# Copies, splits and weight conversions around the first two experts of an attention, MoE and FFN kernel in another order

## The chip, the cores and the metric

The kernel runs on one core of one Trainium2 chip. The metric is the device time of one execution in microseconds (us); three runs of a kernel are shown by their median. The engines are named as in the profile: PE is TensorE, PEld its weight loads, DVE VectorE, ACT ScalarE, POOL GpSimd, SP SyncE, which here issues DMAs.

## The reference

Three layers, one after the other, on 2 x 768 tokens of width 384 (8 heads of 48):

```python
for t in range(S):                                     # attention with a decaying state
    state = alpha[:, :, t, :, None] * state + np.einsum('bhd,bhe->bhde', k[:, :, t], v[:, :, t])
    y[:, :, t] = np.einsum('bhd,bhde->bhe', q[:, :, t], state)
...
expert_idx = np.argmax(x @ w_gate, axis=1)             # one of 8 experts per token, 1536 tokens
h = np.maximum(np.einsum('ecd,edf->ecf', disp, w1), 0.0)   # 384 -> 1024
y = np.einsum('ecf,efd->ecd', h, w2)                       # 1024 -> 384
out[i] = gate_w[i] * y[expert_idx[i], pos[i]]
...
h = x @ w_in                                           # second FFN, 384 -> 2048
g = h * np.tanh(np.log1p(np.exp(np.minimum(h, 20.0))))
return g @ w_out                                       # 2048 -> 384
```

All inputs are float32, except that `w_in` and `w_out` of the second FFN come as 64-bit numbers.

## The kernel before, in words

**Stages.** The attention goes over 12 tiles of 128 tokens. Behind each tile its tokens are routed (their expert, their place in it, the gate), scaled by the gate and scattered into a table `tab` in HBM, sorted by expert. Then come the 8 experts, then the second FFN, whose rows are scattered to the output.

**Splits.** Every float32 operand of a product in the experts and in the second FFN is split in two parts: a high part that ACT copies (`whi` of the weights, `xh` of the tokens, `hh` of the middle layer) and a low part that DVE subtracts (`wlo`, `xl`, `hl`). Each product becomes three: high by high, low by high, high by low.

**Weights.** They come in 72 pieces of 128 x 768. SP loads piece i into a staging tile `st` (`load_to`, up to 14 pieces ahead), ACT writes `whi[i]` (`conv_high`, line L343), DVE writes `wlo[i]` (`conv_low`, L349). Pieces 0 to 63 are the experts' (8 each). Pieces 64 to 71 are the first half of the second FFN; these start as 64-bit numbers and are first turned into float32 in 12 jobs. Job n has two halves: `cvt_a(n)` (an ACT copy `wm` at L198, an ACT check at L233, two DVE operations on `wt` at L201 and L204) and `cvt_b(n)` (one DVE operation at L209 that joins the halves of a word, and the DMA that writes the result to `wi_s` or `wo_s` in HBM, L241). Pieces 64 to 71 are then loaded back from there, and a piece's load stands in the program only when the jobs that write it do: pieces 68 to 71 wait for all 12.

**Steps.** An expert e has 8 steps m; step number e*8+m issues `g1(e, m)`, nine products of 240 columns of the first layer (L1100), and `g2` of three steps earlier, nine products of the second layer (L1117). `g1(e, m)` writes a PSUM bank that it shares with `g1(e, m-2)`, so it waits until DVE's `hl(e, m-2)` (L1105) is done. `xpose(e+1)` transposes the next expert's tokens (PE, L1072) and splits them into `xh` and `xl` (L1089, L1090); `gather(e)` fetches them from the table. `place(e)` loads a register with the expert's offset on the engines that address by it.

**Order.** The order in which the program text issues work is the order on each engine: nothing is sorted afterwards. An instruction that waits holds up all that stands behind it on its engine. The conversion halves are put at steps by two lines, in which `CVT_END` is 45 and 24 halves are spread over the list `free`:

```python
free = [s for s in range(3, E * MF) if s % MF != 5 and (s % MF != 2 or s < MF)]
    job_at.setdefault(free[n * CVT_END // (2 * len(cvt_jobs))], []).append(((cvt_a, cvt_b)[n % 2], n // 2))
```

**The check.** Every attention tile leaves in `chk` how far an iteration converged. `check_tiles` (DVE, L784 and L786: `ok`, then `cm`, a minimum over 12 columns) sums it up, `check_all(cm)` at step 7 transposes `cm` on PE (L791) and reduces it on DVE (L793) to a flag, which with the largest expert's count `mxc` decides on a slow path at the end.

**Second FFN.** `f1(n)` is nine products of 512 columns (L1181), from which ACT and DVE make the gated middle layer: a sigmoid, an arctangent and a sine on ACT (`sigma` L1193, then L1197, L1199) and a product and a split on DVE (`gated`: `p` L1209, high part `big` L1210, low part `big` L1211). `f2` is twelve products of 384 columns (L1224) on it. The loop is `f1(n)`, then `f2` of two blocks earlier. Block 4 is the first whose `f1` takes its weights from piece 68.

Of the kernel before, what the change touches and what calls it, by code (L numbers as in the profile page):

```python
# [10 lines left out]
F32 = mybir.dt.float32  # L11
# [12 lines left out]
def kernel(  # L24
# [309 lines left out]

    low = []

    def conv_high(n):
        while conv_n[0] < min(n, len(pieces)):
            i = conv_n[0]
            load_to(i + 1 + ahead[0])  # L340
            w = wst_t.pop(i)
            w_new(i)
            nc.scalar.activation(out=whi[i], in_=w, func=AF.Copy)  # L343
            low.append((i, w))
            conv_n[0] += 1

    def conv_low(only=None):
        for i, w in [x for x in low if only in (None, x[0])]:
# [15 lines left out]

    with ExitStack() as actx:
        ap_ = actx.enter_context(tc.tile_pool(name="att", bufs=1))
        chk = ap_.tile([128, NTILE], F32, name="chk")
        nc.vector.memset(chk, 0.0)
        neg1 = ap_.tile([128, 1], F32, name="neg1")
        nc.vector.memset(neg1, -1.0)  # L370
# [2 lines left out]
        sel = ap_.tile([128, HP, SW], F32, name="sel")  # L373

        tri_f = ap_.tile([128, 128], F32, name="tri_f")
        seen_f = ap_.tile([128, 128], F32, name="seen_f")
        seen = ap_.tile([128, 128], I32, name="seen")
        io_i = ap_.tile([128, E], I32, name="io_i")
        slot_i = ap_.tile([128, WIN], I32, name="slot_i")
# [1 line left out]
        def route_consts():  # L381
            nc.gpsimd.memset(tri_f, 1.0)
            nc.gpsimd.affine_select(
                out=tri_f, in_=tri_f, pattern=[[1, 128]], compare_op=ALU.is_gt,
                fill=0.0, base=0, channel_multiplier=-1,
            )
            nc.gpsimd.memset(ones, 1.0)
            nc.gpsimd.memset(seen_f, -1.0)
            nc.gpsimd.affine_select(
                out=seen_f, in_=seen_f, pattern=[[1, 128]], compare_op=ALU.is_ge,  # L390
                fill=0.0, base=0, channel_multiplier=-1,
            )
            nc.gpsimd.iota(io_i, pattern=[[-1, E]], base=E - 1, channel_multiplier=0)
            nc.gpsimd.iota(slot_i, pattern=[[1, WIN]], base=(E - 1) * NT, channel_multiplier=0)
            nc.gpsimd.iota(tokid, pattern=[[C, NTILE]], base=0, channel_multiplier=1)

        def route_copies():
            nc.scalar.activation(out=tri, in_=tri_f, func=AF.Copy)
            nc.scalar.activation(out=seen, in_=seen_f, func=AF.Copy)
            nc.scalar.activation(out=down, in_=io_i, func=AF.Copy)  # L400
            nc.scalar.activation(out=firsts, in_=io_i[0:1], func=AF.Copy, scale=float(NT))
            nc.scalar.activation(out=slots, in_=slot_i, func=AF.Copy)
# [111 lines left out]

        def k_scale(i):
            kp = sp.tile([128, HP, C], F32, tag="kp", name="kp")
            nc.vector.scalar_tensor_tensor(
                out=kp[0:R2], in0=heads(kn_t.pop(i))[0:R2], scalar=-1.0 if i == NTILE - 1 else 1.0,
                in1=rt_t.pop(i)[0:R2], op0=ALU.mult, op1=ALU.mult,
            )  # L520
            kp_t[i] = kp

        def q_scale(i):
# [410 lines left out]
        for i in range(1, NTILE - 1):  # L934
            far = i + 2 < NTILE
            carry, carried = (t % NC_B != NC_B - 1 for t in (i, i - 1))
            load_step(i + 3)
            zero_tab(i - 1, 4)
            scores(i)
            mask(i, 0)  # L940
            mask(i, 1)
            decay_er(i + 1)
            if i < 7:
                decay_inv(i + 1)
            if carried:
                state_up(i - 1)
            if i >= 7:
                decay_inv(i + 1)
            if carry:
                k_back(i)  # L950
            else:
                idle(i, 1)
            if i in RANK:
                group_rank_mm(RANK[i])
            x_back(i - 1)
            if not far:
                own(RANK[i])
            if carry:
                k_neg(i)
            if i in (7, 8, 9):  # L960
                put(1 + i // 9)
            elif i < 7:
                decay_check(i + 1)
            if far:
                decay_scan(i + 2)
                decay_ln(i + 2)
                group_lg(i - 1)
                decay_exp(i + 2)
                k_scale(i + 1)
                q_scale(i + 1)  # L970
                if i in (7, 8, 9):
                    put(1)
                group_in(i - 1)
                if i in RANK:
                    own(RANK[i])
            else:
                put(2)
                route(i - 1)
                k_scale(i + 1)
                q_scale(i + 1)  # L980
            if i in EXP:
                group_exp(EXP[i])
            if i in HOT:
                group_hot(HOT[i])
            attend_state(i)
            if not carried:
                idle(i, 1)
            attend_tile(i)
            if not far:
                route_rank_mm(i - 1)  # L990
                route_gate(i - 1)
                route_rank(i - 1)
                route_slot(i - 1)
                count(i)
            if carry:
                state_mm(i)
            x_out(i)
            if not far:
                route_x(i - 1)
                route_c(i - 1)  # L1000
            load_to(PRE.get(i, 0))
# [6 lines left out]
        state_up(i - 1)  # L1008
        mask_last(i, 0)
        x_back(i - 1)  # L1010
        idle(i, 2)
        attend_state(i)
        route(i - 1)
        decay_check(i - 1)
# [26 lines left out]
        low_x = split_x(i)  # L1041
        route_rank(i)
        slot_hot(i)
        low_x()
        route_x(i)
        route_slot(i)
        cm = check_tiles()
        count(i + 1)
        route_c(SLOT1)
        conv_high(ATT - 1)  # L1050
        conv_low(0)
        slot_split()
        del xs_t[0]
        tot = rk[:, E:2 * E]
        nc.tensor.matmul(out=tot, lhsT=ones, rhs=pre[pre_n[0] % 2], start=True, stop=True, skip_group_check=True)


    wr_p.append(main.enter_context(tc.tile_pool(name="wr1", bufs=8)))
# [283 lines left out]
    CVT_END = 45  # L1342
    LATE_AHEAD = 3
    xpose(0, False)
    nc.vector.tensor_reduce(out=mxc, in_=tot, axis=AX.X, op=ALU.max)
    conv_low(2)
    conv_high(ATT)
    scatter(tab, si_last, xg_last, E * NT, "tab")
    gather(1)
    pend = []  # L1350
    job_at = {}

    free = [s for s in range(3, E * MF) if s % MF != 5 and (s % MF != 2 or s < MF)]
    for n in range(2 * len(cvt_jobs)):
        job_at.setdefault(free[n * CVT_END // (2 * len(cvt_jobs))], []).append(((cvt_a, cvt_b)[n % 2], n // 2))
    for e in range(E):
        for m in range(MF):
            step = e * MF + m
            if m == 6:
                off_v[e] = place(e)  # L1360
            g1(e, m)
            pend.append((e, m))
            if len(pend) > LAG:
                pe, pm = pend.pop(0)
                g2(pe, pm)
                if pm == MF - 1:
                    y_out(pe)
            if e == E - 1 and m >= MF - EARLY:
                n = m - MF + EARLY
                (f_head if m < MF - 1 else f1_at)(n)  # L1370
# [3 lines left out]
            for f, n in job_at.get(step, ()):  # L1374
                f(n)
                if f is cvt_b:
                    cvt_load(n + 3)
            if step == 4:
                places()
            if step == 5:  # L1380
                sort_places()
            if step == 7:
                check_all(cm)
                slow_at()
            if step % 4 == 3 and 0 < step // 4 <= NTILE:
                tok_scatter(step // 4 - 1)
# [8 lines left out]
            if step == E * MF - 2:  # L1395
                cvt_flag()
            if m == (5 if e else 6) and e + 1 < E:
                xpose(e + 1)
                if e + 2 < E:
                    gather(e + 2)  # L1400
    for pe, pm in pend:
# [242 lines left out]
```

## Time and profile before

| | |
|---|---|
| median of 3 runs | 421.44 us (421.35 to 422.85) |
| the profiled execution | 421.35 us, of which its span, from the first to the last instruction, is 419.6 us |
| mean granted TensorE clock | 0.996 |
| busy: PE, DVE, ACT, POOL | 406.4, 323.9, 324.5, 58.6 us |
| first expert's first product, second expert's first | 75.43 us, 89.94 us |
| first block of the second FFN whose weights are piece 68 | 221.38 us |

The span leaves 1.75 us of the execution outside. The busy times are sums over the whole span, with a matmul's end modelled, so a busy PE says only that something was in it; where it waits is in the timeline, in the idle time before an instruction and what ended it.

### The profile page before, as it was taken

What the parts mean: (1) busy time and instruction counts of PE and PEld (TensorE: products, weight loads), DVE (VectorE), ACT (ScalarE), POOL (GpSimd) and SP (SyncE); (2) the same over time, 40 slices, a digit from 0 to 9 for tenths busy, and PEclk for the clock granted to TensorE, in tenths of its full rate; (3) what the DMA queues carried; (4) which work ended last, traced back from release to release, by engine and by line L of the source; (5) the groups of instructions that cost most, each with busy time, mean ns of one, the idle gap of its engine ahead of it and who ended that gap; (6) DMA issues with size and microseconds to landing.
All of it is one profiled execution on the core that took longest, in us unless ns stands there. A gap on an engine that the chain in (4) does not pass through costs nothing.

```text
span 419.6 us, 8354 instructions
## 1 busy us (share of the span) xinstructions
PE 406.4 (97%) x3111; PEld 374.5 (89%) x3114; DVE 323.9 (77%) x645; ACT 324.5 (77%) x572; POOL 58.6 (14%) x77
## 2 busy tenths in 40 slices
PE   7899999899999999999999999999999999999993
PEld 3798998899999999999999899989898988889893
DVE  7999997899989888988649877867786775565361
ACT  5889997877868677777499987888788869797630
POOL 5222573101101012100000000000000000012043
PEclk9999999999999999999999999999999999999998
DMA  7999996999999999944525000211110000001022
GB/s 236 351 290 334 347 382 224 352 354 235 341 322 285 303 313 283 287 128 125 187 80 174 15 1 0 52 63 39 37 41 1 0 2 0 2 19 57 2 77 80
DMA packets 50541, 67.31 MB, mean 160 GB/s; under 512 B 5372, under 2 KB 41212, under 8 KB 50492
## 3 DMA queue, kind: packets, MB, share of 16 engines
q1 hardware_dynamic: 48572, 61.97, 47.9%
q0 software_dynamic: 1920, 4.73, 3.1%
q8 instruction: 26, 0.43, 0.4%
q14 instruction: 23, 0.19, 0.1%
HBM read 55.86 MB, written 10.83 MB: 159 GB/s over the span
## 4 chain that ended last, share of the span: by engine, by line
PE 89%; DVE 5%; ACT 2%; issue 1%; DMA 1%; POOL 0%; POOLq 0%; DVEq 0%; ACTq 0%
PE bk L1224 24%; PE bk L1181 24%; PE bk L1117 14%; PE bk L1100 14%; PE bk L537 3%; PE bk L589 2%; PE bk L605 2%; PE bk L578 2%; DVE wlo L349 1%; PE bk L557 1%; PE bk L613 1%; PE bk L1072 1%; DMA an<-in_alpha_t_dram 1%; DVE hl L1105 0%; PE bk L868 0%
## 5 line engine op out<-in xcount | busy, mean ns | idle before, releaser
L349 DVE TENSOR_TENSOR wlo<-st,whi 128x768 fp32r<-128x768 f32 x72 | 68.2, 953 | 12.4 <-ACT whi L343 9.9
L1209 DVE TENSOR_TENSOR p<-p,bk 128x512 f32<-128x512 f32 x48 | 32.8, 683 | 43.6 <-ACT p L1199 43.6
L1224 PE MATMUL bk<-whi,big 128*128 128x384 f32 x240 | 66.4, 337 | 0.0
L343 ACT ACTIVATE whi<-st 128x768 fp32r<-128x768 f32 x72 | 60.1, 841 | 0.0
L1193 ACT ACTIVATE p<-bk 128x512 f32<-128x512 f32 x48 | 28.8, 599 | 32.0 <-PE bk L1181 28.6
L1117 PE MATMUL bk<-hl,whi 128*128 128x240 f32 x192 | 52.9, 276 | 0.0
L1117 PE MATMUL bk<-hh,wlo 128*128 128x240 f32 x192 | 52.7, 275 | 0.0
L1117 PE MATMUL bk<-hh,whi 128*128 128x240 f32 x192 | 52.7, 274 | 0.0
L1224 PEld LDWEIGHTS bk<-whi,big 128*128 128x128 f32 x240 | 44.1, 188 | 1.5
L1104 ACT ACTIVATE hh<-bk 128x240 fp32r<-128x240 f32 x64 | 23.5, 367 | 28.2 <-PE bk L1100 25.3
L108 POOL DMA_INDIRECT out_dram<-acc,srt x12 | 12.2, 1018 | 225.5 <-DVE acc L1248 221.1
L1181 PE MATMUL bk<-x2l,whi 128*128 128x512 f32 x144 | 41.6, 397 | 0.0
L1181 PE MATMUL bk<-x2h,wlo 128*128 128x512 f32 x144 | 41.2, 394 | 0.0
L1181 PE MATMUL bk<-x2h,whi 128*128 128x512 f32 x144 | 41.1, 394 | 0.0
L1224 PE MATMUL bk<-wlo,big 128*128 128x384 f32 x120 | 40.6, 338 | 0.0
L1117 PEld LDWEIGHTS bk<-hl,whi 128*128 128x128 f32 x192 | 36.4, 189 | 0.2 <-DVE hl L1105 0.2
L1117 PEld LDWEIGHTS bk<-hh,whi 128*128 128x128 f32 x192 | 36.3, 189 | 0.0
L1117 PEld LDWEIGHTS bk<-hh,wlo 128*128 128x128 f32 x192 | 36.3, 189 | 0.0
L1100 PE MATMUL bk<-xh,whi 128*128 128x240 f32 x192 | 33.0, 280 | 1.7 <-ACT xh L1089 1.6
L1181 PEld LDWEIGHTS bk<-x2h,wlo 128*128 128x128 f32 x144 | 27.0, 188 | 6.7
L1181 PEld LDWEIGHTS bk<-x2l,whi 128*128 128x128 f32 x144 | 27.0, 188 | 6.4
L1100 PE MATMUL bk<-xl,whi 128*128 128x240 f32 x192 | 32.1, 276 | 0.4 <-DVE xl L1090 0.4
(238 smaller groups left out, 955.4 us busy)
## 6 DMA issues: line engine op xcount, KB each, us to landing
st<-in_w_dram SPq DMA_DIRECT2D x64, 384.0 KB, 7.9
qn<-in_q_t_dram SPq DMA_DIRECT2D x12, 256.0 KB, 5.4
kn<-in_k_t_dram SPq DMA_DIRECT2D x12, 256.0 KB, 7.1
w<-in_w_in_dram SPq DMA_DIRECT2D x6, 512.0 KB, 7.4
w<-in_w_out_dram SPq DMA_DIRECT2D x6, 512.0 KB, 6.4
sd<-in_w_in_dram SPq DMA_DIRECT2D x8, 384.0 KB, 4.1
sd<-in_w_out_dram SPq DMA_DIRECT2D x8, 384.0 KB, 4.7
tab<-zero SPq DMA_DIRECT2D x4, 720.0 KB, 6.5
```

What stands on the lines that cost most here:

```text
L108: r = nc.gpsimd.indirect_dma_start(out=dst[:, :], out_offset=bass.IndirectOffsetOnAxis(ap=idx, axis=0), in_=src, in_offset=None, bounds_ch ...
L343: nc.scalar.activation(out=whi[i], in_=w, func=AF.Copy)
L349: nc.vector.tensor_tensor(out=wlo[i], in0=w, in1=whi[i].bitcast(F32), op=ALU.subtract)
L537: nc.tensor.matmul(out=sc_t[i][r][:, j], lhsT=kp[p, j, :], rhs=qq[p, j, :], start=True, stop=True)
L578: nc.tensor.matmul(out=ot_at(j, r), lhsT=s2f[half(r), j * D:j * D + w], rhs=q2[i % 2][half(r), j, :], start=(j % 2 == 0), stop=False, skip ...
L1100: nc.tensor.matmul(out=hps, lhsT=a[:, kk], rhs=b_[:, kk, :], start=(n == 0), stop=(n == 3 * KD - 1))
L1104: nc.scalar.activation(out=hh, in_=hps, func=AF.Relu)
L1117: nc.tensor.matmul(out=y[n], lhsT=a[:, ns], rhs=b_, start=(m == 0 and t == 0 and n % 2 == 0), stop=(m == MF - 1 and t == 2), skip_group_ch ...
L1181: r = nc.tensor.matmul(out=hps, lhsT=a[:, kk], rhs=b_[:, kk, w0:w0 + wd], start=(n == 0), stop=(n == 3 * KD - 1))
L1193: nc.scalar.activation(out=p, in_=h2_t[b], func=AF.Sigmoid, scale=-1.0)
L1209: nc.vector.tensor_tensor(out=g, in0=g, in1=h2_t.pop(b), op=ALU.mult)
L1224: nc.tensor.matmul(out=o_t[c], lhsT=a[:, ts], rhs=b_, start=(m in (0, MA) and n == 0), stop=(m in (MA - 1, MF2 - 1) and n == 2),)
```

## The change

It changes the order of ACT's copies and of DVE's small operations between the attention and the second expert, shifts all conversion halves by two entries of `free`, and has four small edits in the attention. Part by part:

- ACT copies `whi[2]` between the two gate-scaled copies `xg_lh` and `xg_l` of the last tile, `whi[1]` behind `xh` of the first expert, and `whi[3]` behind step 0. Before, `whi[1]` and `whi[2]` stood together in front of `xh`.
- `check_tiles` moves from in front of the first expert to step 7, right ahead of the transposes of its result; `mxc` moves to step 4; the product for `tot` moves behind `g1(0, 0)`.
- `xpose(1)` stands ahead of step 6's weight copies, and `place(0)` a step later.
- The conversion halves start at step 5's place in `free` instead of step 3's: the first, `cvt_a(0)`, goes from step 3 to 6, the last, `cvt_b(11)`, from step 60 to 63 (the last step).
- GpSimd builds the mask `seen` as int32 at once, and ACT's copy to int32 is gone; `k_scale` is a plain product for tiles 1 to 10; tile 9's gate stands ahead of tile 11's `q_scale`; one of the last tile's two keep-busy products, which nothing reads, is gone.

```diff
@@ -334,15 +334,17 @@
+    def high(i):
+        load_to(i + 1 + ahead[0])
+        w = wst_t.pop(i)
+        w_new(i)
+        nc.scalar.activation(out=whi[i], in_=w, func=AF.Copy)
+        low.append((i, w))
+        conv_n[0] += 1
+
     def conv_high(n):
         while conv_n[0] < min(n, len(pieces)):
-            i = conv_n[0]
-            load_to(i + 1 + ahead[0])
-            w = wst_t.pop(i)
-            w_new(i)
-            nc.scalar.activation(out=whi[i], in_=w, func=AF.Copy)
-            low.append((i, w))
-            conv_n[0] += 1
+            high(conv_n[0])
...
-            nc.gpsimd.memset(seen_f, -1.0)
+            nc.gpsimd.memset(seen, -1)
             nc.gpsimd.affine_select(
-                out=seen_f, in_=seen_f, pattern=[[1, 128]], compare_op=ALU.is_ge,
-                fill=0.0, base=0, channel_multiplier=-1,
+                out=seen, in_=seen, pattern=[[1, 128]], compare_op=ALU.is_ge,
+                fill=0, base=0, channel_multiplier=-1,
             )
...
-            nc.scalar.activation(out=seen, in_=seen_f, func=AF.Copy)
...
-            nc.vector.scalar_tensor_tensor(
-                out=kp[0:R2], in0=heads(kn_t.pop(i))[0:R2], scalar=-1.0 if i == NTILE - 1 else 1.0,
-                in1=rt_t.pop(i)[0:R2], op0=ALU.mult, op1=ALU.mult,
-            )
+            kn, rt = heads(kn_t.pop(i))[0:R2], rt_t.pop(i)[0:R2]
+            if i < NTILE - 1:
+                nc.vector.tensor_tensor(out=kp[0:R2], in0=kn, in1=rt, op=ALU.mult)
+            else:
+                nc.vector.scalar_tensor_tensor(out=kp[0:R2], in0=kn, scalar=-1.0, in1=rt, op0=ALU.mult, op1=ALU.mult)
...
@@ -977,6 +978,7 @@
                 put(2)
                 route(i - 1)
                 k_scale(i + 1)
+                route_gate(i - 1)
                 q_scale(i + 1)
...
                 route_rank_mm(i - 1)
-                route_gate(i - 1)
                 route_rank(i - 1)
...
-        idle(i, 2)
+        idle(i, 1)
...
@@ -1041,18 +1042,16 @@
         low_x = split_x(i)
         route_rank(i)
         slot_hot(i)
+        high(2)
         low_x()
         route_x(i)
         route_slot(i)
-        cm = check_tiles()
+        conv_low(0)
         count(i + 1)
         route_c(SLOT1)
-        conv_high(ATT - 1)
-        conv_low(0)
         slot_split()
         del xs_t[0]
         tot = rk[:, E:2 * E]
-        nc.tensor.matmul(out=tot, lhsT=ones, rhs=pre[pre_n[0] % 2], start=True, stop=True, skip_group_check=True)
...
@@ -1342,21 +1341,20 @@
     xpose(0, False)
-    nc.vector.tensor_reduce(out=mxc, in_=tot, axis=AX.X, op=ALU.max)
     conv_low(2)
-    conv_high(ATT)
+    high(1)
     scatter(tab, si_last, xg_last, E * NT, "tab")
     gather(1)
     pend = []
     job_at = {}
 
-    free = [s for s in range(3, E * MF) if s % MF != 5 and (s % MF != 2 or s < MF)]
+    free = [s for s in range(5, E * MF) if s % MF != 5 and (s % MF != 2 or s < MF)]
     for n in range(2 * len(cvt_jobs)):
         job_at.setdefault(free[n * CVT_END // (2 * len(cvt_jobs))], []).append(((cvt_a, cvt_b)[n % 2], n // 2))
     for e in range(E):
         for m in range(MF):
             step = e * MF + m
-            if m == 6:
+            if m == (6 if e else 7):
                 off_v[e] = place(e)
             g1(e, m)
...
+            if step == 6:
+                xpose(1)
...
+            if step == 0:
+                nc.tensor.matmul(out=tot, lhsT=ones, rhs=pre[pre_n[0] % 2], start=True, stop=True, skip_group_check=True)
             if step == 4:
+                nc.vector.tensor_reduce(out=mxc, in_=tot, axis=AX.X, op=ALU.max)
                 places()
             if step == 5:
                 sort_places()
             if step == 7:
-                check_all(cm)
+                check_all(check_tiles())
                 slow_at()
...
             if m == (5 if e else 6) and e + 1 < E:
-                xpose(e + 1)
+                if e:
+                    xpose(e + 1)
```

What the instructions' order shows. A name's number is the tile's own; lines are those of each kernel, so a line of the changed one is off by one to two.

First ACT between the attention and the first expert. `xg_lh` and `xg_l` are the last tile's scaled tokens (their high part and the whole), `xh` is the first expert's split. Before:

```order
L838 ACTIVATE xg_lh_180<-bk3_89,gt_1307 128x384
L764 ACTIVATE xg_l1_169<-bk3_89,gt_1307 128x384
L343 ACTIVATE whi1_1326<-st1_791 128x768
L343 ACTIVATE whi2_1329<-st2_793 128x768
L1089 ACTIVATE xh_1361<-bk0_86 128x2x240
L1089 ACTIVATE xh_1361<-bk1_87 128x240
L343 ACTIVATE whi3_1375<-st3_883 128x768
L1104 ACTIVATE hh_1393<-bk2_88 128x240
```

With the change:

```order
L839 ACTIVATE xg_lh_179<-bk3_89,gt_1304 128x384
L341 ACTIVATE whi2_1312<-st2_791 128x768
L765 ACTIVATE xg_l1_168<-bk3_89,gt_1304 128x384
L1088 ACTIVATE xh_1350<-bk0_86 128x2x240
L1088 ACTIVATE xh_1350<-bk1_87 128x240
L341 ACTIVATE whi1_1359<-st1_789 128x768
L1103 ACTIVATE hh_1377<-bk2_88 128x240
L341 ACTIVATE whi3_1385<-st3_881 128x768
```

Two copies of weights no longer stand between `xg_l` and `xh`: one is ahead of `xg_l`, the other behind `xh`.

Then DVE at the second expert's split `xl`, up to `cmx`, which reads the transposed `cm`. With the change it reads:

```order
L1089 TENSOR_TENSOR xl_1552<-bk0_86,xh_1551 128x2x240
L1089 TENSOR_TENSOR xl_1552<-bk1_87,xh_1551 128x240
L351 TENSOR_TENSOR wlo9_1560<-st9_1083,whi9_1559 128x768
L201 TENSOR_SCALAR wt_1563<-w64_1344 128x512
L204 SCALAR_TENSOR_TENSOR wt_1563<-w64_1344,wt_1563 128x512
L1142 TENSOR_LOAD meta_i_106
L1104 SCALAR_TENSOR_TENSOR hl_1593<-bk3_89,hh_1592 128x240
L351 TENSOR_TENSOR wlo10_1608<-st10_1085,whi10_1607 128x768
L209 SCALAR_TENSOR_TENSOR wt_1563<-w64_1344,wt_1563 128x512
L785 TENSOR_SCALAR ok_1615<-chk_127 128x12
L787 TENSOR_REDUCE cm_1617<-ok_1615 128x1
L794 TENSOR_REDUCE cmx_1620<-bk7_93 1x1
```

Before, `ok` and `cm` stood here, between the first expert's last routing and its split:

```order
L839 SCALAR_TENSOR_TENSOR xg_ll_181<-bk3_89,gt_1307,xg_lh_180 128x384
L775 CAST si_all_107<-sl_l11_172 128x1
L784 TENSOR_SCALAR ok_1318<-chk_127 128x12
L786 TENSOR_REDUCE cm_1320<-ok_1318 128x1
L672 TENSOR_REDUCE pre0_140<-oh_all_139 128x8
L349 TENSOR_TENSOR wlo0_1273<-st0_710,whi0_1272 128x768
L1090 TENSOR_TENSOR xl_1362<-bk0_86,xh_1361 128x2x240
```

And PE at the transposes of `cm`, with the semaphores waited for. Before:

```order
L1117 MATMUL bk5_91<-hh_1480,whi5_1431 128x240
L1117 MATMUL bk5_91<-hh_1480,wlo5_1432 128x240
L1117 MATMUL bk5_91<-hl_1481,whi5_1431 128x240
L791 MATMUL bk7_93<-ident_96,cm_1320 1x128
L1100 MATMUL bk2_88<-xh_1585,whi8_1531 128x240 [waits DVE_49,Activation_49]
```

With the change:

```order
L1116 MATMUL bk5_91<-hh_1466,whi5_1423 128x240
L1116 MATMUL bk5_91<-hh_1466,wlo5_1424 128x240
L1116 MATMUL bk5_91<-hl_1467,whi5_1423 128x240
L792 MATMUL bk7_93<-ident_96,cm_1617 1x128 [waits DVE_49]
L1099 MATMUL bk2_88<-xh_1551,whi8_1514 128x240 [waits Activation_49]
```

`ok` and `cm` have moved behind `xl` of the second expert, two splits of weights (pieces 9 and 10), the first conversion job (`wt`, three operations), and `hl`; PE's transposes, which waited for nothing, now wait for DVE, and the second expert's first product stands behind them.

Last, SP's queue and DVE's at the end of the experts: `wo_s` is written by the last conversion job, `st68` to `st71` are the loads of pieces 68 to 71. SP before:

```order
L274 DMA sd2_3403<-in_w_in_dram 128x3x256
L241 DMA wo_s_119<-wt_3337 128x512
L272 DMA sd3_3523<-in_w_out_dram 128x768
L331 DMA st68_3525<-wi_s_118 128x3x256
L331 DMA st69_3527<-wo_s_119 128x2x384
```

SP with the change:

```order
L274 DMA sd2_3394<-in_w_in_dram 128x3x256
L272 DMA sd3_3518<-in_w_out_dram 128x768
L241 DMA wo_s_119<-wt_3422 128x512
L331 DMA st68_3614<-wi_s_118 128x3x256
L331 DMA st69_3616<-wo_s_119 128x2x384
```

DVE with the change, from the low part of piece 67 on:

```order
L351 TENSOR_TENSOR wlo67_3521<-st67_3047,whi67_3520 128x768
L254 SCALAR_TENSOR_TENSOR slow_i_109<-bk5_91,slow_f_110 1x1
L1104 SCALAR_TENSOR_TENSOR hl_3536<-bk3_89,hh_3535 128x240
L209 SCALAR_TENSOR_TENSOR wt_3422<-w64_3020,wt_3422 128x512
L1208 TENSOR_TENSOR p_3462<-p_3462,bk0_86 128x512
L1209 CAST big_3602<-p_3462 128x512
```

DVE before, from the same row on:

```order
L349 TENSOR_TENSOR wlo67_3534<-st67_3056,whi67_3533 128x768
L254 SCALAR_TENSOR_TENSOR slow_i_109<-bk5_91,slow_f_110 1x1
L1105 SCALAR_TENSOR_TENSOR hl_3549<-bk3_89,hh_3548 128x240
L1209 TENSOR_TENSOR p_3467<-p_3467,bk0_86 128x512
L1210 CAST big_3613<-p_3467 128x512
```

The join of the last job (`wt`) now stands behind the low part of piece 67 and the last `hl`, ahead of the second FFN's gated product `p`; before, it is not in this stretch.

## Rows read from the trace of the kernel before

**Rows 1.** Page, part 4: chain that ended last, share of the span by engine.
```profile
PE 89%; DVE 5%; ACT 2%; issue 1%; DMA 1%; POOL 0%; POOLq 0%; DVEq 0%; ACTq 0%
```

**Rows 2.** Two stretches: length, busy PE, PEld, DVE, ACT, POOL; granted clock, DMA share, GB/s.
```profile
75.41:93.70 18.29, 17.80 (x150) 17.23 (x151) 16.99 (x36) 13.77 (x28) 0.98 (x1) 1.00 1.05 364
221.40:240.00 18.60, 18.60 (x93) 16.66 (x93) 17.14 (x31) 17.96 (x26) 0.00 (x0) 1.00 0.33 107
```

**Rows 3.** Timeline, 70 to 78 us: start, duration, engine, line, operation, idle before.
```profile
72.88 0.58 ACT L764 ACTIVATE xg_l<-bk,gt 128x384 f32<-128x384 f32 x1 [0.69 <-DVE xg_ll L839]
73.02 0.17 DVE L786 TENSOR_REDUCE cm<-ok 128x1 f32<-128x12 f32 x1
...
73.27 0.50 PE L846 MATMUL bk<-hot_last,xg_ll 128*128 128x240 f32 x3
...
73.36 1.56 ACT L343 ACTIVATE whi<-st 128x768 fp32r<-128x768 f32 x2
...
74.82 0.82 ACT L1089 ACTIVATE xh<-bk 128x480 fp32r<-128x480 f32 x2
...
75.43 0.64 PE L1100 MATMUL bk<-xh,whi 128*128 128x240 f32 x3 [1.65 <-ACT xh L1089]
```

**Rows 4.** Timeline of TensorE's weight loads and products, 84 to 94 us.
```profile
85.08 0.41 PEld L1100 LDWEIGHTS bk<-xh,whi 128*128 128x128 f32 x3 [0.23 <-DVE hl L1105]
...
87.21 0.78 PE L1072 MATMUL bk<-ident,xs 128*128 128x128 f32 x6
...
89.85 0.27 PE L791 MATMUL bk<-ident,cm 128*1 128x128 f32 x1
```

**Rows 5.** Chain that ended last, 84 to 96 us: start, duration, what.
```profile
91.97 1.01 PE bk L1117 x9
```

**Rows 6.** Timeline of ScalarE, 85 to 96 us.
```profile
88.99 0.82 ACT L1089 ACTIVATE xh<-bk 128x480 fp32r<-128x480 f32 x2
...
89.94 0.87 ACT L343 ACTIVATE whi<-st 128x768 fp32r<-128x768 f32 x1
...
92.36 1.57 ACT L343 ACTIVATE whi<-st 128x768 fp32r<-128x768 f32 x2
```

**Rows 7.** Timeline of VectorE, 85 to 96 us.
```profile
85.81 0.69 DVE L209 SCALAR_TENSOR_TENSOR wt<-w,wt 128x512 uint32<-128x512 uint32 x1
...
91.77 0.95 DVE L349 TENSOR_TENSOR wlo<-st,whi 128x768 fp32r<-128x768 f32 x1
92.64 0.42 DVE L201 TENSOR_SCALAR wt<-w 128x512 uint32<-128x512 uint32 x1
```

**Rows 8.** Groups of VectorE to 75 us: busy, mean ns | idle before.
```profile
L517 DVE SCALAR_TENSOR_TENSOR kp<-kn,rt 112x512 f32<-112x512 f32 x11 | 8.5, 769 | 0.0
```

**Rows 9.** Timeline of SyncE's DMA issues, 195 to 212 us.
```profile
203.32 0.34 SPq L241 DMA_DIRECT2D wo_s<-wt  x1
```

**Rows 10.** DMA issues of 204.1 to 205 us: KB each, us to landing.
```profile
st<-wi_s SPq DMA_DIRECT2D x1, 384.0 KB, 4.1
```

**Rows 11.** Timeline of VectorE, 212 to 232 us.
```profile
215.85 0.38 DVE L1105 SCALAR_TENSOR_TENSOR hl<-bk,hh 128x240 fp32r<-128x240 f32 x1
...
226.58 0.69 DVE L1211 TENSOR_TENSOR big<-p,big 128x512 fp32r<-128x512 f32 x1
```

**Rows 12.** Timeline of ScalarE, 212 to 232 us.
```profile
218.49 0.86 ACT L343 ACTIVATE whi<-st 128x768 fp32r<-128x768 f32 x1
```

**Rows 13.** Timeline of TensorE, 212 to 224 us.
```profile
221.38 0.85 PE L1181 MATMUL bk<-x2h,whi 128*128 128x512 f32 x3
```

**Rows 14.** Chain that ended last, 218 to 232 us.
```profile
227.84 2.11 PE bk L1224 x12
```

**Rows 15.** Timeline of TensorE at the program's start and end.
```profile
1.27 5.71 PE L799 MATMUL bk<-busy 128*128 128x512 bf16 x14 [1.27 <-DVE busy L138]
...
412.23 0.34 PE L1224 MATMUL bk<-whi,wlo 128*128 128x384 f32 x1
```

**Rows 16.** The same view as Rows 2, of 0.5 us behind TensorE's last product.
```profile
416.00:416.50 0.50, 0.00 (x0) 0.00 (x0) 0.00 (x0) 0.00 (x0) 0.00 (x0) 0.50 0.06 22
```

More of the change, by code (lines that the diff above doesn't have):

```diff
@@ L366 @@
         ap_ = actx.enter_context(tc.tile_pool(name="att", bufs=1))
-        chk = ap_.tile([128, NTILE], F32, name="chk")
+        chk = const.tile([128, NTILE], F32, name="chk")
         nc.vector.memset(chk, 0.0)
@@ L375 @@
         tri_f = ap_.tile([128, 128], F32, name="tri_f")
-        seen_f = ap_.tile([128, 128], F32, name="seen_f")
         seen = ap_.tile([128, 128], I32, name="seen")
```

## The prediction

> **What bounds the kernel now.** I read four kinds of view, from the whole to the single wait. First the chain that ended last, over the whole span: 89% of it is PE [rows 1]. So an edit pays only where PE waits, and costs only where it makes PE wait. Then the busy times of two stretches which the change touches [rows 2]. From the first expert's split to 93.70 us PE is busy 17.80 of 18.29 us, but DVE 16.99: DVE is nearly as full as PE. At the head of the second FFN PE is busy 18.60 of 18.60, ACT 17.96 and DVE 17.14: whatever makes ACT late there by more than some tenths cannot be caught up. Third, the timeline around the first expert's start: PE waits 1.65 us for ACT's `xh`, the longest wait in this part [rows 3]. Fourth, the timelines around the second expert's start and the second FFN's head, for the duration of each instruction that stands in a new place [rows 4 to 7, 9 to 14].
>
> **The first expert's start: a gain.** ACT's `xg_l` starts at 72.88 after 0.69 us of idling, which ended with DVE's `xg_ll`. Then come two weight copies, 1.56 us, then `xh` at 74.82, and PE starts at 75.43, 0.61 us behind the start of `xh` [rows 3]. With the change one weight copy fits into the idle time and the other follows `xh`. `xh` then waits for the later of `xg_l` (72.88 + 0.58 = 73.46) and the product it copies, PE's L846, which ends at 73.27 + 0.50 = 73.77 [rows 3]. `xh` reads two banks and the first is done a little earlier, so I take 73.6. That is 74.82 - 73.6 = 1.2 us less. A second, small one: the weight load at 85.08 waited 0.23 us for DVE's `hl`, behind conversion work that now comes later [rows 4]. Together PE should reach the transposes of `xpose(1)` about 1.4 us sooner: at 87.21 - 1.4 = 85.8, and those of `cm` at 89.85 - 1.4 = 88.45 [rows 4].
>
> **The second expert's start: a new wait.** Before, `cm` was made at 73.02 [rows 3] and PE's transposes of it waited for nothing. Now `cm` stands in DVE's order behind the second expert's `xl`, the low parts of pieces 9 and 10 and the whole of the first conversion job, and PE's transposes wait for it, with the second expert's first product queued behind them. When is `cm` ready? I work it out three ways.
>
> By the chain of ACT's work: the six transposes take 0.78 us [rows 4], so `xh` starts at 85.8 + 0.78 = 86.6 and takes 0.82; from the start of the weight copy behind it to the start of the copy of piece 10 it took 92.36 - 89.94 = 2.42 us, in which lie the same instructions (`wm`, the check, `hh`); the copy takes 0.87 [rows 6]. That ends at 90.7. Behind it on DVE the low part takes 92.64 - 91.77 = 0.87 and the join 0.69 [rows 7], `ok` and `cm` about 0.17 each [rows 3]: 92.6 us.
>
> By DVE's queue, at its former pace: its order from the first `xl` to the end of the stretch at 93.70 is nearly the same, less the two `wt` operations of the second job (0.42 and one like the join's 0.69 [rows 7]), plus `ok` and `cm` (0.35). From the new start of 74.2 (75.43 - 1.2) that gives 74.2 + 18.29 - 1.11 + 0.35 = 91.7 [rows 2, 3]. If DVE idled nowhere, it would be 74.2 + 16.99 - 1.11 + 0.35 = 90.4, the lower bound. The upper one is the former pace without any gain: 93.70 - 1.11 + 0.35 = 92.9.
>
> I take 92.2, between the first two, as the hand-overs of the chain overlap by a tenth each. PE then waits from 88.45 to 92.2, about 3.75 us. The first g1 of the second expert ends 0.1 (the transposes) + 1.01 (nine products, as in [rows 5]) later, at 93.3. Before, it ended at 91.97, where the next nine products begin [rows 5]. Net of all that was gained before it: **+1.35 us**, with bounds of -0.45 (at 90.4) and +2.1 (at 92.9).
>
> **The second FFN's head: a later write.** The last job wrote its half of `wo_s` at 203.32, and the load of piece 68 was issued behind it, long before ACT wanted it at 218.49 [rows 9, 12]. Now the join stands on DVE behind the last `hl`, which runs at 215.85 for 0.38 [rows 11]: it takes 0.69 [rows 7] and ends at about 216.9. SP's queue holds the write, then the load: at 0.34 for an issue [rows 9], the load starts at 217.3, and such a load took 4.1 us to land [rows 10]: 221.4. ACT waits there, with the sigmoids of the next blocks queued behind its copy: 221.4 - 218.49 = 2.9 us late [rows 12]. The copy ends at 221.4 + 0.86 = 222.3. Block 4's f1 on PE wants it at 221.38 [rows 13]: 0.9 us of waiting, a first, certain part. But ACT stays 2.8 us late, and with it DVE's gated values of block 2, whose low part started at 226.58 and took 0.69 [rows 11]: that now ends at 226.58 + 0.69 + 2.8 = 230.05. `f2` of block 2 started at 227.84 [rows 14], and its third product reads that low part; products of 384 columns are 2.11 / 12 = 0.18 apart [rows 14], so it can start no earlier than 230.05 - 0.35 = 229.7, 1.85 later. As the first two products read the high part, done 0.7 before, they go ahead and the third waits, some 0.2 more. **+2.05 us**, with bounds of +0.9 (only f1's wait counts, DVE's values come in time) and +2.9 (all of ACT's lateness). ACT's 17.96 busy of 18.60 [rows 2] cannot absorb it. All other conversions are two entries later too, but their pieces are wanted tens of us later, and nothing waits for them.
>
> **Edits costed at nothing.** The mask's ACT copy lay in the first microseconds, while PE ran 14 keep-busy products from 1.27 to 6.98 [rows 15]. That cover gone, it would save some tenths. `k_scale` took 0.77 us on average [rows 8]; a plain product of like size takes 0.69 [rows 11], so ten of them save at most 0.8 us if all lay on the chain; DVE never idled before them, but the chain is PE's. I take 0, with 0.8 as the bound. Tile 9's gate, ahead of `q_scale`, moves 0.69 us of DVE work behind two tiny operations: a scatter issued some tenths earlier, nobody waiting: 0, with 0.3 either way. One keep-busy product fewer: 5.71 / 14 = 0.41 us at the low clock of the start [rows 15], half of it at full clock: at most -0.2, taken as 0. `place(0)` and `xpose(1)` a little earlier or later lie in the chain above.
>
> **The sum.** +1.35 + 2.05 = +3.4 on the profiled execution of 421.35, which lies 0.09 under the median of 421.44: 424.8 us, slower by 0.8%. The bounds alone give 421.8 to 426.4. A change of under 0.5%, 2.1 us, could not be told from none here.
>
> **Rivals.**
> *A. The clock falls in the new wait.* At the program's end TensorE's last product began at 412.23 [rows 15], and the granted clock was 0.50 in the half microsecond from 416.00 [rows 16]; the longest pause inside the experts, 1.65 us, left it at 1.00 [rows 2, 3]. The new wait of 3.75 us would be longer than any pause in the experts before. At the program's start, coming from rest, 14 products took 5.71 us, 0.41 each, at the lower level [rows 15]. If as long a stretch behind the wait ran at 1.2 instead of 2.4 GHz, half of it, 2.85 us, would be lost: 424.8 + 2.85 = 427.6. Against it: the wait may end before, and by DVE's lower bound it lasts only 2 us. The Trainium skill (TensorE: Matmul & The Clock Gate, Part 1: The HAM clock gate (the "warmup" mystery)) says that an idle TensorE falls to half clock and returns only after sustained activity; the trace's start and end agree with it, 0.41 us a product and 0.50.
> *B. `cm` is ready in time.* If DVE, relieved of conversions in steps 3 to 5, got to `cm` by 88.45, PE would not wait at all. The stage would then gain 1.4, and the 1.0 us that PE waited between 89.85 and 91.97 (2.12 less the 0.1 and 1.01 of work [rows 4, 5]): -2.4, so 421.35 - 2.4 + 2.05 = 421.0, not slower. It decides at 88.45; DVE's busy time alone puts `cm` at 90.4.
> *C. The late load is hidden.* If only f1's 0.9 of waiting or less stays at the head, and PE makes some of it up, the sum is 421.35 + 1.35 = 422.7. For it: PE runs three blocks ahead of the gated values. Against it: ACT has 0.64 us of slack in 18.6.
> *B and C together*: 421.35 - 2.4 = 418.95, faster.
> *D. The second expert's tokens land late.* `gather(1)` is issued little earlier, while `xpose(1)` comes 1.4 us earlier; if it lands at the old time, the chain to `cm` starts later by about 1: 425.8.
>
> **How the numbers follow.** My forecast 0.48, A 0.22, C 0.12, D 0.08, B 0.05, B and C together 0.05. Time: 424.8. Range 422.2 to 428.0: it takes in A, D and C, and leaves out B, both together and a little at the ends. Faster by over 0.5% (under 419.3): 0.05. Within 0.5% (419.3 to 423.5): B, C and a small part of my own case's lower bound, 0.20. Slower: 0.75.
>
> **What the profile after would show.** First product of the first expert near 74.2, idle in front of it near 0.4. PE idle 3 to 4 us ahead of the transposes of `cm`, released by DVE, and the granted clock of the stretch behind it 1.00 (A: below). The second expert's second stage starts near 93.3. ACT idle some 3 us ahead of piece 68's copy, with a DMA as its releaser, PE idle about 0.9 ahead of block 4's f1 and about 1 ahead of block 2's f2. The prediction is wrong if `cm`'s transposes wait for under 2 us, or if the load of piece 68 is issued well before 217.

## The result and the profile after

The changed kernel took 427.61 us (median of 17 runs, 425.81 to 433.10) against 421.63 us of the kernel before in 17 runs of the same series: the ratio is 1.0121, with a 95% interval of 1.0098 to 1.0144. It is slower, by 6.0 us of the medians and by 5.1 us by the ratio, in which one slow run of 433.1 us is not counted. The profiled execution lies at the upper end, 429.2 us with a span of 427.4. A second series on another chip gave 1.0114 (1.0088 to 1.014) with a median of 425.88 us, and its profile, 425.79 us with a span of 424.0, is the one that is read here first: the kernel before was profiled on the same chip at 421.37 us, span 419.5, and its rows lie within 0.3 us of [rows 3, 4, 13].

The timeline of TensorE in that second profile of the changed kernel (start, duration, engine, line, operation, idle time before and what ended it):

```profile
73.99 0.64 PE L1099 MATMUL bk<-xh,whi 128*128 128x240 f32 x3 [0.67 <-ACT xh L1088]
...
85.58 0.78 PE L1071 MATMUL bk<-ident,xs 128*128 128x128 f32 x6
...
92.35 0.27 PE L792 MATMUL bk<-ident,cm 128*1 128x128 f32 x1 [3.97 <-DVE cm L787]
92.38 0.86 PE L1099 MATMUL bk<-xh,whi 128*128 128x240 f32 x3
```

The first row answers to the last of [rows 3]: PE starts 1.4 us sooner than at 75.43, and waits 0.67 instead of 1.65. `xpose(1)` starts at 85.58 instead of 87.21 [rows 4]: 1.6 us gained. Then the transposes of `cm`, which waited for nothing before, wait 3.97 us for DVE. The first products behind them take 0.86 us for three; before the change such a group took 0.57 or 0.58 where nothing held it up. VectorE in front of it, in the same profile:

```profile
90.46 0.96 DVE L351 TENSOR_TENSOR wlo<-st,whi 128x768 fp32r<-128x768 f32 x1 [0.16 <-ACT whi L341]
91.33 0.68 DVE L209 SCALAR_TENSOR_TENSOR wt<-w,wt 128x512 uint32<-128x512 uint32 x1
91.93 0.17 DVE L785 TENSOR_SCALAR ok<-chk 128x12 f32<-128x12 f32 x1
92.13 0.17 DVE L787 TENSOR_REDUCE cm<-ok 128x1 f32<-128x12 f32 x1
```

Two operations of 0.17 us stand behind a split of 0.96 and a join of 0.68. `cm` ends at 92.3. The same stretch by windows (length, busy PE, PEld, DVE, ACT, POOL with their instructions, granted clock, DMA share, GB/s):

```profile
92.00:94.00 2.00, 1.65 (x9) 1.65 (x10) 0.83 (x6) 0.00 (x0) 0.97 (x1) 0.63 1.11 360
94.00:96.00 2.00, 2.00 (x12) 2.00 (x12) 0.72 (x2) 1.45 (x3) 0.00 (x0) 0.52 1.02 353
96.00:98.00 2.00, 2.00 (x20) 2.00 (x19) 1.81 (x3) 1.09 (x3) 0.00 (x0) 1.00 1.04 387
```

The reader is to see the clock column, 0.63 and 0.52, and beside it the number of products: 12 in two busy microseconds, then 20. PE's busy time alone does not show it. Read as time at 1.00 and at 0.50, the two values are 1.5 and 1.9 us at the low clock, from 92.5 to 95.9: the clock fell just behind the end of the wait.

At the second FFN's head, SyncE's issues, then ScalarE's copy of piece 68, then TensorE's blocks 3 and 4 and the second layer of block 2, in the same profile:

```profile
220.08 0.33 SPq L241 DMA_DIRECT2D wo_s<-wt  x1
220.46 0.43 SPq L331 DMA_DIRECT2D st<-wi_s  x1
```

```profile
223.79 0.85 ACT L341 ACTIVATE whi<-st 128x768 fp32r<-128x768 f32 x1 [1.97 <-DMA st<-wi_s]
```

```profile
220.40 0.85 PE L1180 MATMUL bk<-x2h,whi 128*128 128x512 f32 x3
...
224.69 0.96 PE L1180 MATMUL bk<-x2h,whi 128*128 128x512 f32 x3
...
231.65 0.44 PE L1223 MATMUL bk<-whi,big 128*128 128x384 f32 x1 [0.39 <-DVE big L1209]
```

Blocks 3 and 4 in the kernel before, on the same chip:

```profile
217.30 0.85 PE L1181 MATMUL bk<-x2h,whi 128*128 128x512 f32 x3
...
221.50 0.85 PE L1181 MATMUL bk<-x2h,whi 128*128 128x512 f32 x3
```

The write that stood at 203.32 [rows 9] is issued at 220.08, the load behind it at 220.46, and ACT waits 1.97 us for it. Block 4's products begin 4.29 us behind those of block 3 (220.40) instead of 4.20, a mere 0.1, and the larger loss comes a block later, at 231.65, where DVE's gated values are late. (This `f2` of block 2 stands behind `f1` of block 5: the loop's `f2` is three blocks behind its `f1`, not two.) The load that ACT waits for reads `wi_s`, and the six writes of `wi_s` were issued from 92.0 to 180.2:

```profile
L241 SPq DMA_DIRECT2D wi_s<-wt x6: 332/338/344, 92.0 to 180.2; - x6
```

So the load is late by its place in the program, behind the last write, which goes to `wo_s`, and not for want of its data. No run put it ahead of that write.

The first profile has the same three waits and one more. ScalarE there, TensorE's transposes of `cm`, and the windows of the same stretch:

```profile
79.27 0.84 ACT L341 ACTIVATE whi<-st 128x768 fp32r<-128x768 f32 x1 [2.32 <-DMA tab<-xg_l,si_all]
```

```profile
94.32 0.37 PE L792 MATMUL bk<-ident,cm 128*1 128x128 f32 x1 [3.97 <-DVE cm L787]
```

```profile
92.00:93.00 1.00, 0.00 (x0) 0.00 (x0) 0.83 (x2) 0.40 (x1) 0.00 (x0) 1.00 1.08 379
93.00:94.00 1.00, 0.00 (x0) 0.00 (x0) 1.00 (x3) 0.00 (x0) 0.00 (x0) 0.64 1.08 384
94.00:96.00 2.00, 1.68 (x9) 1.68 (x10) 0.80 (x5) 0.00 (x0) 0.87 (x1) 0.50 1.21 330
96.00:98.00 2.00, 2.00 (x11) 2.00 (x11) 0.63 (x2) 1.36 (x3) 0.11 (x1) 0.50 0.89 166
98.00:100.00 2.00, 2.00 (x11) 2.00 (x11) 1.60 (x2) 0.48 (x1) 0.00 (x0) 0.50 1.03 299
```

ACT waits 2.32 us for a scatter from the last attention tiles: its landing took 6.7 us in this execution and 3.2 in the other. The low clock lasts from 93.3 to 100 us instead of from 92.5 to 95.9. These two make up 3.0 of the 3.4 us between the two profiles: the transposes of `cm` start 20.29 us behind the first product (74.03) instead of 18.36, which is 1.9 us for the scatter, and from them to block 3 of `f1` it takes 1.1 us more (the table below), which is left for the clock.

### The profile page after: what moved, and what is told of

The parts are those of the page before. It is cut to its first block, busy times and chain, and to the rows that moved or that the text cites. A ratio compares the mean times of both kernels' runs of the same rounds, so it can differ in the third digit from the quotient of the medians.

```text
span 427.4 us, 8356 instructions
## 1 busy us (share of the span) xinstructions
PE 409.1 (96%) x3113; PEld 376.5 (88%) x3113; DVE 325.0 (76%) x645; ACT 324.3 (76%) x571; POOL 59.0 (14%) x77
## 4 chain that ended last, share of the span: by engine, by line
PE 89%; DVE 3%; DMA 3%; ACT 2%; issue 1%; SPq 0%; POOL 0%; POOLq 0%; ACTq 0%; DVEq 0%
PE bk L1223 23%; PE bk L1180 23%; PE bk L1116 15%; PE bk L1099 14%; PE bk L538 3%; PE bk L606 3%; PE bk L590 3%; PE bk L579 2%; DMA tab<-xg_l,si_all 2%; DMA an<-in_alpha_t_dram 1%; PE bk L558 1%; PE bk L1071 1%; PE bk L614 1%; DVE wlo L351 1%; DVE pt L472 1%; ACT whi L341 1%
## 5 line engine op out<-in xcount | busy, mean ns | idle before, releaser
L1099 PE MATMUL bk<-xh,whi 128*128 128x240 f32 x192 | 33.9, 286 | 1.9 <-issue 1.2
L1104 DVE SCALAR_TENSOR_TENSOR hl<-bk,hh 128x240 fp32r<-128x240 f32 x64 | 25.8, 403 | 10.7 <-ACT hh L1103 10.6
L1099 PE MATMUL bk<-xh,wlo 128*128 128x240 f32 x192 | 32.6, 279 | 0.2 <-DVE wlo L351 0.2
```

What stands on the lines that cost most here:

```text
L1099: nc.tensor.matmul(out=hps, lhsT=a[:, kk], rhs=b_[:, kk, :], start=(n == 0), stop=(n == 3 * KD - 1))
L1104: nc.vector.scalar_tensor_tensor(out=hl, in0=hps, scalar=0.0, in1=hh.bitcast(F32), op0=ALU.max, op1=ALU.subtract)
```

## The experiments

Every profile can be cut in three by two rows of PE: from the start to the first product of the first expert, from there to the first product of f1 of block 3 (the one ahead of block 4), and from there to the end of the span. The first part differs by nearly 4 us between chips and executions of the same code up to there (73.99 to 77.94 with the change, 75.43 to 78.64 in the kernel before's code), so it tells little of the change; the other two hold still to 0.5 us where their code is the same, but for the changed kernel's first profile. The table is worked out from the profiles' rows and spans, in us.

| kernel | first product at | to block 3 of f1 | to the end | ratio to before |
|---|---|---|---|---|
| before, first profile | 75.43 | 141.75 | 202.4 | |
| changed, first profile | 74.03 | 149.44 | 203.9 | 1.0121 |
| before, again | 75.56 | 141.74 | 202.2 | |
| changed, again | 73.99 | 146.41 | 203.6 | 1.0114 |
| check early | 77.80 | 141.65 | 203.95 | 0.9995 |
| last job early | 77.94 | 146.32 | 202.2 | 1.0071 |
| PE busy in the wait | 76.42 | 144.79 | 203.5 | 1.0055 |
| both back | 76.78 | 141.65 | 202.5 | 0.9957 |
| both back, attention as before | 74.46 | 141.64 | 202.2 | 0.9955 |
| copies' order alone | 74.46 | 141.78 | 202.3 | 0.9973 |
| check late alone | 78.94 | 146.39 | 202.2 | 1.0134 |
| jobs' shift alone | 78.64 | 141.11 | 203.45 | 1.0027 |
| both back, second series | 76.70 | 141.63 | 202.1 | 0.9961 |
| both back, attention as before, second series | 77.56 | 141.63 | 202.3 | 0.9968 |

**The check early again.** In the changed kernel:

```diff
         route_slot(i)
+        cm = check_tiles()
         conv_low(0)
...
-                check_all(check_tiles())
+                check_all(cm)
```

> Only the check stands early again; the shifted conversions and all else stay. If the wait for cm (3.97 us in the profile after) and the half clock behind it (2.9 us lost) are what costs at the second expert's start, this gives back all but the part that DVE owes anyway: 423.2 us (421.4, plus 1.5 at the second FFN's head, plus some tenths), clock 1.00 from 92 to 100 us. Rival, that DVE is behind and PE only waits in another place: 425 or more.

Measured: 425.0 us against 424.97 of before on the same chip, 0.9995 (0.9982 to 1.0007). The level of that chip is 3 us higher, so the ratio is compared: from 1.0121 to 0.9995 are 5.3 us, where the expectation had 4.4. The transposes no longer wait, and no window behind them is below a clock of 1.00:

```profile
92.03 0.27 PE L792 MATMUL bk<-ident,cm 128*1 128x128 f32 x1
92.06 0.58 PE L1100 MATMUL bk<-xh,whi 128*128 128x240 f32 x3
```

The middle part of the table falls from 146.41 to 141.65, as before the change. The rival, that PE would wait for DVE in another place, falls. The loss at the second FFN's head is still there (203.95); that the whole comes out at the kernel before all the same fits the first expert's earlier start, which the expectation did not count.

**The last job early.** In the changed kernel, so that the last join stands at step 60 again:

```diff
-    CVT_END = 45
+    CVT_END = 43
```

> Only the spread of the conversion jobs ends two entries sooner, so that the last join stands at step 60 as before the change. If the late write of wo_s costs the 1.5 us that PE loses at the second FFN's head, 1.5 less than the changed kernel: 426.1. Rival, that the head's loss has another origin or is hidden: 427.6, no change.

Measured: 428.2 us, 1.0071 (1.0047 to 1.0096), 0.4 to 0.5% below the changed kernel's ratio, some 2 us. Block 4 follows block 3 by 4.18 us, and no row of ACT waits for a load there:

```profile
224.26 0.86 PE L1180 MATMUL bk<-x2h,whi 128*128 128x512 f32 x3
...
228.44 0.85 PE L1180 MATMUL bk<-x2h,whi 128*128 128x512 f32 x3
```

The last part is 202.2, as before the change, while the wait for `cm` is still there (3.98 us). The head's loss is that of the late write and the loads behind it.

**PE busy in the wait.** In the changed kernel; the products' results are read by nobody:

```diff
-                check_all(check_tiles())
+                cm = check_tiles()
+                for _ in range(32):
+                    nc.tensor.matmul(out=bk[2][:, 0:WIN], lhsT=busy[:, 0:128], rhs=busy[:, 0:WIN], start=True, stop=True)
+                check_all(cm)
```

> 32 products of 240 columns that nothing reads stand ahead of the transposes of cm, about 3.2 us of work inside the 3.97 us wait. If the clock's fall in that wait costs 2.9 us on top of the wait, the clock stays 1.00 and the time is 427.6 - 2.9 = 424.7. Rival, that DVE and ACT are the bound behind the wait and the slow products are hidden: 427.6.

Measured: 427.26 us, 1.0055 (1.0033 to 1.0077). The rows of TensorE, and the windows behind them:

```profile
90.65 3.45 PE L1388 MATMUL bk<-busy 128*128 128x240 bf16 x32
94.78 0.27 PE L792 MATMUL bk<-ident,cm 128*1 128x128 f32 x1 [0.68 <-DVE cm L787]
```

```profile
94.00:96.00 2.00, 1.32 (x13) 1.22 (x12) 1.26 (x6) 0.00 (x0) 0.48 (x1) 1.00 1.09 366
96.00:98.00 2.00, 2.00 (x20) 2.00 (x19) 1.17 (x2) 1.84 (x3) 0.50 (x1) 1.00 1.08 306
```

`cm` is ready as late as in the changed kernel, 18.36 us behind the first product in both (94.78 - 76.42 and 92.35 - 73.99), but the clock stays at 1.00 and 20 products pass in two microseconds at once. The middle part is 144.79: 1.6 us less than 146.41, 3.1 more than 141.7. The 1.6 are the clock's, the rest the wait's. In the changed kernel's first profile the clock's part is 1.6 + 1.1 = 2.7 us by the same reading. By ratio the gain is 0.6 to 0.7% (1.0114 or 1.0121 against 1.0055), near the expectation's 0.7% (2.9 us of 427.6); the intervals are too wide to tell 1.6 us from 2.7.

**Both back.** The first two edits together, all else of the change kept.

> The check early and the last job early, all else of the change kept. If the two costs add, 427.6 - 4.4 - 1.5 = 421.7, the kernel before within 0.2%. Rival, that the earlier start of the first expert then shows at the end: 420.0.

Measured: 423.2 us, 0.9957 (0.9942 to 0.9972), and 0.9961 (0.9947 to 0.9975) in a second series. This is faster than both kernels by more than the expectation's first line and matches its rival: what remains of the change is a gain of 0.4%.

**Before and after once more, copies alone, and without the attention's edits.** The first two are the kernels as they are. The third is the kernel before with:

```diff
         slot_hot(i)
+        high(2)
         low_x()
...
-        conv_high(ATT - 1)
         conv_low(0)
...
     conv_low(2)
-    conv_high(ATT)
+    high(1)
```

The fourth is "both back" with the mask by an ACT copy, `k_scale` and tile 9's gate as before, and `idle(i, 2)`.

> The kernel before once more, for a profile from the same chip as the next three. If its time differs from chip to chip in the attention alone (the runs of before had a median of 421.63 on one and 424.97 on another), its first expert's product starts some 3 us later than at 75.43 and everything behind it keeps its distances; rival, that it loses behind the attention too.

> The changed kernel once more. In its first profile ACT waited 2.3 us for piece 4's copy until a scatter landed, 6.7 us after its issue; the four variants profiled since show no such wait. If that is chance of one execution, the profile is without it, the wait for cm and the half clock are there, and the ratio to before is 1.010 to 1.013. Rival, that it belongs to the changed kernel: the wait of over 2 us is there again.

> The kernel before with the order of the weight copies around xh alone. If the 1.2 us by which PE starts earlier reach the end: 0.997 of before. Rival, that DVE, busy 16.99 of 18.29 us there, takes it back by the second expert: 1.000.

> The variant with the check early and the last job early (0.9957 of before), and with the mask, k_scale, tile 9's gate and the keep-busy product as before. If those four edits are worth nothing: 0.996 again. Rival, that they bring what that variant gained: 1.000.

Measured: the kernel before, one run, 421.37 us, so this chip was at the first level and answers nothing on the other's. The next group answers it in part: the check late alone and the jobs' shift alone have the same code as the kernel before up to the first expert's product, but for the check's two operations in the one, on a chip at 424.47 us, and there that product starts at 78.94 and 78.64 instead of 75.56. The attention's product at L860, not far ahead of it, starts at 73.30 and 72.95 instead of 69.87, so the level is lost in the attention. Why it differs between chips is open. The changed kernel 425.88, 1.0114, without the wait for the scatter: that wait was one execution's, and what made the landing 6.7 us is not settled (GpSimd took 1.73 us over that scatter's issue instead of 0.99; nothing was tried on it). The copies alone 420.59, 0.9973 (0.9957 to 0.9988): the first product moves from 75.56 to 74.46 and the middle part stays at 141.78, so the gain reaches the end. Without the attention's edits 420.09, 0.9955 (0.9936 to 0.9974): the same ratio as with them on the other chip. TensorE's first product in the two:

```profile
74.46 0.64 PE L1102 MATMUL bk<-xh,whi 128*128 128x240 f32 x3 [0.66 <-ACT xh L1091]
```

```profile
74.46 0.64 PE L1101 MATMUL bk<-xh,whi 128*128 128x240 f32 x3 [0.67 <-ACT xh L1090]
```

**Single parts on the kernel before.** The check late alone (`chk` goes to a pool that lives until step 7, as in the changed kernel):

```diff
-        chk = ap_.tile([128, NTILE], F32, name="chk")
+        chk = const.tile([128, NTILE], F32, name="chk")
...
-        cm = check_tiles()
...
-                check_all(cm)
+                check_all(check_tiles())
```

the jobs' shift alone:

```diff
-    free = [s for s in range(3, E * MF) if s % MF != 5 and (s % MF != 2 or s < MF)]
+    free = [s for s in range(5, E * MF) if s % MF != 5 and (s % MF != 2 or s < MF)]
```

and "both back" with and without the attention's edits again, all four on one chip.

> The kernel before with the check alone moved to step 7. In DVE's order cm then stands behind the low part of piece 10 and the second job's two wt operations, which ended at 93.70 before; with its own 0.35 us it is ready at 94.05, while PE asks at 89.85. PE waits about 4.2 us, the second expert's first nine products end 3.2 us later than at 91.97, and the clock falls as in the changed kernel (1.6 us): 1.011 of before, all of the changed kernel's loss without its other parts. Rival, that the wait needs the shifted conversions to arise: 1.000 to 1.003.

> The kernel before with the conversion jobs alone two entries of the list later. If the late write of wo_s costs 1.4 us at the second FFN's head and nothing else comes of the shift: 1.003. Rival, that DVE, relieved before the second expert, gives PE an earlier start there that pays for it: 1.000.

> The variant with check and last job early once more, on the same chip as the next one: 0.995 to 0.996. First product of the first expert some 0.4 us earlier than in the next run if the attention's edits are worth something, at the same time if not.

> The same without the four edits in the attention: the same ratio within 0.1% if they are worth nothing at the end; 0.1% higher if they are worth 0.4 us.

Measured: the check late alone 1.0134 (1.0113 to 1.0156). It makes the whole loss of the middle part by itself, 146.39, with a wait as long:

```profile
97.61 0.37 PE L791 MATMUL bk<-ident,cm 128*1 128x128 f32 x1 [4.11 <-DVE cm L786]
```

The profiled execution, 429.23 us, is the fastest of its five. The others took 0.7 to 1.9 us more at mean clocks of 0.986 to 0.990 instead of 0.993, so their low stretch may have been longer; no profile shows it.

The jobs' shift alone 1.0027 (1.001 to 1.0043): the last part is 203.45, 1.25 us more than before, and the middle part 141.11, 0.6 less, so both sides of that expectation are there and the loss is the larger. Its row of ACT:

```profile
223.29 0.84 ACT L343 ACTIVATE whi<-st 128x768 fp32r<-128x768 f32 x1 [2.10 <-DMA st<-wi_s]
```

With and without the attention's edits 0.9961 and 0.9968 (0.9953 to 0.9983): the intervals overlap almost wholly. The first product, by which the expectation would have it decided, starts 0.86 us earlier with them (76.70 against 77.56), and on the earlier chip 0.47 earlier (73.99 in the changed kernel against 74.46 without them). Each of these is one execution, and the times do not follow: the medians are 423.30 and 423.32 us. Whether the four edits gain some tenths is left open.

## Why the prediction was right, and where it was off

The direction was right, the range held the time, and the mechanisms of the sum are there in the rows, at the places named. The time of the likeliest case, 424.8, was too low by 2.8 us, because that case left out rival A: the clock fell, and A's own figure, 427.6, is the median that was measured. That it fits to a tenth is luck in part: A took 2.85 us for the clock from the program's start, and the profiles show 1.6 and 2.7; the first pair of profiles differs by 7.8 us with a scatter's wait of 1.9 in it, the second by 4.5, and the ratio 1.0121 stands for 5.1.

The terms, against the two profiles of one chip (span 419.5 before, 424.0 after, +4.5):

- *The first expert's start.* Forecast: first product at 74.2 and `xpose(1)` at 85.8. Measured 73.99 and 85.58. The copies' order alone brings 1.1 us of it (75.56 to 74.46); the other 0.5 is there only with the attention's edits (73.99), one execution against two.
- *The wait for `cm`.* Forecast: ready at 92.2, a wait of 3.75 us. Measured 92.3 and 3.97. Net of the gain, forecast +1.35; measured 3.1 us at block 3 of f1 (220.40 - 217.30), of which the clock is 1.6 by the run with PE kept busy: +1.5 without it.
- *The clock.* Taken as nothing in the likeliest case, 2.85 in rival A. Measured 1.6 us in this profile and 2.7 in the first, where the low clock lasted until 100 us. This is the step that failed. Its chance, 0.22, was too small: in all four profiles with this wait whole (the two of the changed kernel, the last job early, the check late alone) the granted clock behind it is near 0.5, and in none of the others. What spoke against it, that DVE's busy time alone would end the wait after 2 us, was a bound that DVE's queue never came near.
- *The second FFN's head.* Forecast +2.05, measured +1.4 (203.6 - 202.2). Mis-sized in the load: taken at 4.1 us to land [rows 10], it let ACT begin 3.3 us behind its issue (220.46 to 223.79), so ACT waited 2.0 us and not 2.9. With this the first part, f1's wait of 0.9, nearly vanished (0.1), and what stayed was the gated values' lateness, as argued.
- *Edits at nothing.* The attention's four edits: 0 was taken, and no difference was found in the times.

Rival B, `cm` in time, was far off: the transposes of `cm` start 18.36 us behind the first product in every profile of the changed kernel's order with the check late, but the one with the scatter's wait. C and D did not show: ACT did wait for the load and did not make it up, and no row of PE or ACT waited for the second expert's tokens. The first profile's scatter wait was in no case of the prediction.

## What to carry to other kernels

Before a small operation is moved to where its result is used, read what stands ahead of it in its engine's queue there: two operations of 0.17 us made PE wait 4 us because a 0.96 us split and a conversion stood before them, and PE's next product stood behind the transposes. A result that is early anyway should stay early. When a wait of some microseconds on PE is forecast, price the slower products behind it as part of the likeliest case, not as a rival; and look for what stands behind the last of a list of jobs, here the loads that are issued behind the last job's write, before the list is shifted as a whole.

## What the runs showed of the hardware

The granted clock fell to 0.5 towards the end of every wait of about 4 us of TensorE, or just behind it, in four profiles (3.97, 3.97, 3.98 and 4.11 us), and stayed there for 3 to 6 us of busy products; 32 products of 240 columns in the same wait kept it at 1.00. The Trainium skill (TensorE: Matmul & The Clock Gate, Part 1: The HAM clock gate (the "warmup" mystery)) says that the throttled state is the default and activity releases it; these runs agree with it. Not expected was how much the length of the low stretch differs between executions of one program, 3.4 us in one profile (92.5 to 95.9) and near 7 in another (93.3 to 100), with products in it from 94.3.

The same indirect scatter landed after 3.2 us in one execution and 6.7 in another of the same program, and by the profile a later ACT copy waited 2.32 us for it. And the same kernel ran 3 us longer on one chip than on another (424.97 against 421.63 for the kernel before), so only ratios to the kernel before on the same chip are compared here.
